# Retention and a bilinear FFN on one core: the first q load issued as two transfers of three and five heads

## The chip, the cores and the metric

The kernel runs on one core of a Trainium2 chip. The metric is device time in microseconds, the median of several executions. Beside it there is one profiled execution, whose span runs from its first to its last instruction.

## What is computed

Two stages follow each other. The first is a retention layer: for each of 8 batches and 8 heads, scores of q against k, multiplied by a causal decay, times v. The second takes the result as tokens of 512 features and runs a bilinear feed-forward network (FFN) over them.

```python
scores = scale * np.matmul(q, k.transpose(0, 1, 3, 2))    # q, k, v: (8, 8, 576, 64) float32
gamma = 1.0 - 2.0 ** (-5.0 - np.arange(H))
Dmat = np.where(rel >= 0, gamma[:, None, None] ** rel, 0.0)
attn = np.matmul(scores * Dmat, v)
x = attn.transpose(0, 2, 1, 3).reshape(B * S, H * D)      # (4608, 512)
out = ((x @ w_a) * (x @ w_b)) @ w_out                     # w_a, w_b: (512, 1536), w_out: (1536, 512)
```

Inputs and output are float32 in device memory; the products run in bfloat16, and the loads convert q, k and the weights on the way.

## The kernel before

The 4,608 tokens are worked off in blocks of 512. For each block the FFN makes, by 12 slices F of the hidden features, two products `pa` and `pb` (`ffn_ab`, L416 to L446: four products each per slice, over the four chunks of 128 input features), ACT copies `pa` to `ha`, DVE multiplies it with `pb` into `hT`, and `ffn_out` (L476) or, for block 0, `ffn_out_parts` (L458) multiplies `hT` with `wo_sb` and stores the rows. The retention of later tokens is laid between the FFN's products by a list of due times (L774 to L806), so that TensorE (PE) always has something to do.

The first 512 tokens can't be hidden in that way: there is no FFN work before them. They are handled in two units u = 0 and 1 of 256 tokens each, by functions whose names begin with `fresh_`. One load brings 256 tokens of q or k for all 8 heads: partition p gets tokens 2p and 2p+1, and for each head these two rows are one piece of 128 numbers, so one load has 128 x 8 pieces. PE then transposes by pairs of heads (`fresh_transposed`, L533), sixteen 64-wide transposes for all of q, which go through the heads in order; DVE scales the transposed q by the decay `qs0` (L669), ACT and DVE copy the transposed k (L673, L674), and PE makes scores, masks being applied by DVE, then the state and the second stage (`fresh_stage2`, L622), whose result is copied into `xT` (L646, L647) for the FFN.

All engines run their own instructions in program order. The order on GpSimd, which issues nearly all loads, is written out by hand at L161 to L171:

```python
    load_fresh_v(0, 0, 4, nc.sync)        # issued by SyncE
    load_fresh_qk(0)                      # q, then k, of tokens 0 to 255
    ramp(idx[:, 0:512], ...); ramp(posf[:, 0:4], ...); ramp(posf[:, 4:4 + MID + 1], ...)
    load_fresh_v(0, 4, 8, nc.gpsimd)
    ramp(posf[:, 4 + MID + 1:NPOS], ...)
    load_fresh_qk(1)                      # q, then k, of tokens 256 to 511
    load_fresh_v(1, 0, 8, nc.gpsimd)
    load_w(0, 128)                        # two wa and two wb loads
    load_w(128, 384)
```

The `ramp` calls make index tables on GpSimd. DVE waits for them: from `posf` and `idx` come the decay of v (`make_vs`, L195), the identity that the transposes multiply with (L211), and the masks `keep2` (`make_keep2`, L214, called at L668). ACT makes `qs0` (L206) and part of `qs` (`make_qs`, L232) from them.

PE's own order at the start is: twelve products on zeros (`idle_products`, L662), which keep it busy while the first data is on the way; the transposes of q of unit 0; two more such products; the transposes of k of unit 0; scores, state and sums of unit 0 with more such products between; the transposes of q of unit 1, one product on zeros, the transposes of k of unit 1 (L688); the second stage of unit 0; and then the FFN's first slice on tokens 0 to 255 (L698), interleaved with unit 1.

A load by GpSimd reports on one of eight semaphores in turn. From the ninth on, GpSimd waits before issuing a load until the load eight places before it has landed. In the instruction order of before this concerns the weight loads from the second `load_w` half on: the first `wb_sb` load waits for q of unit 0, the next one for k of unit 0, and the two `wb_sb` loads of `load_w(128, 384)` for k and v of unit 1.

Of the kernel before, what the change touches and what calls it, by code (L numbers as in the profile page):

```python
# [18 lines left out]
def kernel(  # L19
# [23 lines left out]
    nc = tc.nc  # L43

    B, H, S, D = q.shape
# [91 lines left out]
    def load_fresh_qk(u):  # L137
        t = [nat.tile([128, 2, DM], BF16, tag="qk", name="fqk")
             for _ in (0, 1)]
        for w, src in ((0, q), (1, k)):  # L140
            nc.gpsimd.dma_start(  # L141
                t[w].rearrange("p a b -> p (a b)").rearrange(
                    "p (h x) -> p h x", h=H),
                src[0, :, 256 * u:256 * u + 256, :].rearrange(
                    "h (p e) d -> p h (e d)", e=2))
        fresh[u] = [x.rearrange("p a b -> p (a b)").rearrange(
            "p (h e d) -> p h e d", h=H, e=2) for x in t]

# [11 lines left out]

    load_fresh_v(0, 0, 4, nc.sync)  # L161
    load_fresh_qk(0)
    ramp(idx[:, 0:512], [[1, 512]], 0, 0)
    ramp(posf[:, 0:4], [[1, 2], [256, 2]], 0, 2)
    ramp(posf[:, 4:4 + MID + 1], [[128, MID + 1]], 0, 1)
    load_fresh_v(0, 4, 8, nc.gpsimd)
    ramp(posf[:, 4 + MID + 1:NPOS], [[128, PER - MID - 1]], 64, 1)
    load_fresh_qk(1)
    load_fresh_v(1, 0, 8, nc.gpsimd)
    load_w(0, 128)  # L170
# [685 lines left out]
```

## Time and profile before

| | us |
|---|---|
| median of 5 runs | 327.53 (326.73 to 328.17) |
| the profiled execution, in all | 327.53 |
| its span | 325.7 |
| granted TensorE clock, mean | 1.000 |

The shares of busy time of the five engines, PE ahead of all, are shown with the prediction. A page of the profile gives busy time by engine, the span in 40 slices, the DMA queues, the chain of work that ended last, and the costliest groups of instructions. The timeline lists instructions by start and length; in brackets stands how long the engine was idle before and what ended that idleness. For a load that GpSimd issues, the length is that of the issue, and the landing of its data comes later.

What the early part looks like, as the timeline has it: PE's products on zeros run from 1.19 to 6.08 us, the transposes of q of unit 0 from 6.01, those of k of unit 0 from 7.70, scores from 8.80, transposes of q of unit 1 from 10.65, of k of unit 1 from 12.85, the second stage of unit 0 from 13.41, and the FFN's first product from 14.97. On the whole 23.34 MB move through GpSimd's queue and 16.95 MB through SyncE's.

### The profile page before, as it was taken

The numbers are of one execution on the slowest core, as the hardware profiler recorded it, in microseconds if no ns is written. First come the engines' busy times: TensorE is split into PE (matmuls) and PEld (weight loads), VectorE is DVE, ScalarE is ACT, GpSimd is POOL, SyncE is SP. The second block draws the span as 40 slices with busy tenths as digits, with TensorE's granted clock in tenths as the row PEclk, the third lists the DMA queues.
The fourth block names the chain that finished last, engine by engine and source line by source line (L and its number), as shares of the span: only waits on it lengthen the run. The fifth ranks groups of instructions, "written<-read, shape, count | busy, mean of one in ns | idle before, by whom it ended". The sixth has DMA issues, their size and how long they took to land.

```text
span 325.7 us, 8850 instructions
## 1 busy us (share of the span) xinstructions
PE 319.4 (98%) x3745; PEld 170.9 (52%) x3745; DVE 165.8 (51%) x329; ACT 119.3 (37%) x256; POOL 145.7 (45%) x181
## 2 busy tenths in 40 slices
PE   7899999999999999999999999999999999999996
PEld 3577757886444554455445544545444544544443
DVE  6774445856445744473636364446445634534321
ACT  5737624545034432342334143414332333313321
POOL 8696889592770565056702680098008200000000
PEclk9999999999999999999999999999999999999999
DMA  9999999999999099919991999289937850011002
GB/s 141 199 166 180 180 228 272 174 152 118 200 190 146 13 185 188 137 31 154 170 141 30 150 179 140 53 131 157 164 67 96 145 89 0 32 69 32 2 32 97
DMA packets 117383, 40.94 MB, mean 126 GB/s; under 512 B 104224, under 2 KB 110624, under 8 KB 117344
## 3 DMA queue, kind: packets, MB, share of 16 engines
q0 software_dynamic: 81824, 23.34, 69.0%
q1 hardware_dynamic: 35376, 16.95, 26.6%
q8 instruction: 29, 0.48, 0.6%
q10 hardware_dynamic: 144, 0.10, 0.1%
q14 instruction: 10, 0.08, 0.1%
HBM read 37.75 MB, written 9.44 MB: 145 GB/s over the span
## 4 chain that ended last, share of the span: by engine, by line
PE 94%; POOL 2%; DMA 2%; issue 0%; ACT 0%; POOLq 0%; ACTq 0%
PE pa L433 29%; PE pb L433 29%; PE po L497 25%; PE po L466 3%; DMA wa_sb<-in_moe_w_a_dram 2%; PE o L333 2%; PE o L386 2%; PE sc L361 2%; PE kv L294 1%; POOL fqk L141 1%; PE po L486 1%; PE tp L275 1%; POOL vf L131 0%; PE fo L628 0%; POOL idx L151 0%
## 5 line engine op out<-in xcount | busy, mean ns | idle before, releaser
L443 DVE TENSOR_TENSOR hT<-ha,pb 128x512 bf16<-128x512 bf16 (+1 forms) x123 | 76.4, 622 | 95.7 <-PE pb L433 88.8
L433 PE MATMUL pa<-xT,wa_sb 128*128 128x512 bf16 (+1 forms) x516 | 113.8, 345 | 0.3 <-DMA wa_sb<-in_moe_w_a_dram 0.2
L433 PE MATMUL pb<-xT,wb_sb 128*128 128x512 bf16 (+1 forms) x516 | 113.7, 344 | 0.0
L442 ACT CAST ha<-pa 128x512 bf16<-128x512 f32 (+1 forms) x123 | 65.5, 533 | 115.3 <-PE pa L433 114.7
L497 PE MATMUL po<-wo_sb,hT 128*128 128x512 bf16 x372 | 83.3, 379 | 0.0
L256 POOL TENSOR_TENSOR vb<-vf,vs_all 128x512 bf16<-128x512 f32 x30 | 30.8, 1042 | 101.8 <-PE o L333 94.9
L433 PEld LDWEIGHTS <-wb_sb 128*128 128x128 bf16 x516 | 50.4, 98 | 43.1
L433 PEld LDWEIGHTS <-wa_sb 128*128 128x128 bf16 x516 | 49.4, 98 | 42.3 <-DMA wa_sb<-in_moe_w_a_dram 0.5
L497 PEld LDWEIGHTS <-hT 128*128 128x128 bf16 x372 | 35.5, 98 | 41.8
L110 POOL DMA_DIRECT2D vf<-in_v_dram x36 | 31.6, 881 | 0.1
L102 POOL DMA_DIRECT2D qk<-in_q_dram x36 | 30.9, 866 | 1.2 <-DMA wo_sb<-in_moe_w_out_dram 1.1
L102 POOL DMA_DIRECT2D qk<-in_k_dram x36 | 30.9, 863 | 0.9 <-DMA wo_sb<-in_moe_w_out_dram 0.6
L316 ACT CAST sbf<-s 128x256 bf16<-128x256 f32 x56 | 22.6, 405 | 13.3 <-DVE s L307 5.4
L307 DVE TENSOR_TENSOR s<-kv,s 128x256 f32<-128x256 f32 x49 | 20.7, 423 | 11.7 <-PE kv L294 9.5
L453 DVE COPY osb<-po 128x512 f32<-128x512 f32 x17 | 11.7, 690 | 28.0 <-PE po L497 28.0
L406 DVE TENSOR_TENSOR xT<-o,qs 128x512 bf16<-128x512 f32 x32 | 20.5, 682 | 6.5 <-PE o L333 6.3
L451 ACT COPY osb<-po 128x512 f32<-128x512 f32 x18 | 10.5, 583 | 33.6 <-PE po L497 31.1
L370 DVE TENSOR_TENSOR sT<-sc,keep 128x512 bf16<-128x512 f32 x32 | 20.7, 682 | 0.0
L350 ACT CAST seen<-o 128x64 bf16<-128x64 f32 x16 | 3.4, 212 | 27.8 <-PE o L333 27.8
L333 PE MATMUL o<-qkT,sbf 64*64 64x64 bf16 x456 | 12.2, 196 | 0.0
L333 PEld LDWEIGHTS <-sbf 64*64 64x64 bf16 x456 | 8.4, 106 | 6.6 <-issue 5.9
L466 PE MATMUL po<-wo_sb,hT 128*128 128x512 bf16 x48 | 11.4, 380 | 0.0
(81 smaller groups left out, 150.7 us busy)
## 6 DMA issues: line engine op xcount, KB each, us to landing
vf<-in_v_dram POOLq DMA_DIRECT2D x29, 256.0 KB, 4.7
out_dram<-osb SPq DMA_DIRECT2D x29, 256.0 KB, 4.1
qk<-in_k_dram POOLq DMA_DIRECT2D x28, 128.0 KB, 5.7
qk<-in_q_dram POOLq DMA_DIRECT2D x28, 128.0 KB, 6.3
out_dram<-osb SPq DMA_DIRECT2D x12, 128.0 KB, 4.6
vf<-in_v_dram POOLq DMA_DIRECT2D x8, 128.0 KB, 5.5
wa_sb<-in_moe_w_a_dram POOLq DMA_DIRECT2D x4, 192.0 KB, 6.6
wb_sb<-in_moe_w_b_dram POOLq DMA_DIRECT2D x4, 192.0 KB, 7.2
```

Source lines behind the costliest of these rows:

```text
L102: nc.gpsimd.dma_start(t[r0:r0 + n, w, :].rearrange("p (h d) -> p h d", h=H), src[b, :, s0:s0 + n, :].rearrange("h s d -> s h d"))
L110: nc.gpsimd.dma_start(t[r0:r0 + n, :].rearrange("p (h d) -> p h d", h=H), v[b, :, s0:s0 + n, :].rearrange("h s d -> s h d"))
L256: eng.tensor_tensor(vb.rearrange("p (h d) -> p h d", h=H), vf.rearrange("p (h d) -> p h d", h=H), vs[:, i % PER, :].unsqueeze(2).to_broadc ...
L307: nc.vector.tensor_tensor(new, ps[s][:, ci], last_sum[0], op=ALU.add)
L316: nc.scalar.copy(sb, new)
L333: nc.tensor.matmul(o[s][half(c), ci, j, :], state_of.get(2 * i + s, zero_state)[half(r), p, :], qkt_of[i][half(r), 0, p, half(s)], start=s ...
L370: nc.vector.tensor_tensor(sT[:, r].rearrange("p n c t -> p (n c) t"), sc[r].rearrange("p n c t -> p (n c) t"), keep.unsqueeze(1).to_broadc ...
L433: nc.tensor.matmul((pa, pb)[w][:, t:t + step], (wa_sb, wb_sb)[w][:, c, fs], xT[:, c, tok0 + t:tok0 + t + step], start=(c == 0 and t == 0), ...
L442: nc.scalar.copy(ha[:, 0:n], pa[:, 0:n])
L443: nc.vector.tensor_tensor(hT[:, F, off:off + n], ha[:, 0:n], pb[:, 0:n], op=ALU.mult)
L466: nc.tensor.matmul(po[u], hT[:, F, u * 128:(u + 1) * 128], wo_sb[:, F, :], start=(F == 0), stop=(F == NF - 1))
L497: nc.tensor.matmul(po, hT[:, F, u * 128:(u + 1) * 128], wo_sb[:, F, :], start=(F == 0), stop=(F == NF - 1))
```

## The change

`load_fresh_qk(u)` issued one load of q and one of k, each for all 8 heads. Now the load of q for unit 0 is made of two, for heads 0 to 2 and for heads 3 to 7, issued one after the other from GpSimd into the two parts of the same tile. The load of k for unit 0 and both loads of unit 1 stay whole.

```diff
         for w, src in ((0, q), (1, k)):
-            nc.gpsimd.dma_start(
-                t[w].rearrange("p a b -> p (a b)").rearrange(
-                    "p (h x) -> p h x", h=H),
-                src[0, :, 256 * u:256 * u + 256, :].rearrange(
-                    "h (p e) d -> p h (e d)", e=2))
+            cuts = (0, 3, H) if (u, w) == (0, 0) else (0, H)
+            for h0, h1 in zip(cuts, cuts[1:]):
+                nc.gpsimd.dma_start(
+                    t[w].rearrange("p a b -> p (a b)")[
+                        :, 128 * h0:128 * h1].rearrange(
+                            "p (h x) -> p h x", h=h1 - h0),
+                    src[0, h0:h1, 256 * u:256 * u + 256, :].rearrange(
+                        "h (p e) d -> p h (e d)", e=2))
```

In the instruction orders of the two kernels this is one more load on GpSimd, as its second, ahead of k. PE's first transpose of q waits for the first of the two loads and its sixth for the second. The semaphores of all later loads of GpSimd move on by one place, and each load still waits for the one eight places before it. The orders on PE, DVE, ACT and SyncE are otherwise the same.

## The prediction

> **What bounds the kernel now.** I read the page's first part, then the chain of waits in order of time, then GpSimd's timeline, PE's waits, and last the stretches with DMA share and rate. PE is busy 98% of the span, and in the chain nothing but PE stands between 15 us and the end. So only the start can move the time: when PE gets its first FFN product.
>
> ```profile
> PE 319.4 (98%) x3745; PEld 170.9 (52%) x3745; DVE 165.8 (51%) x329; ACT 119.3 (37%) x256; POOL 145.7 (45%) x181
> ```
>
> The chain of waits (start, length, what) at the start:
>
> ```profile
> 1.26 1.95 POOL fqk L141 x2
> ...
> 4.98 1.71 POOL fqk L141 x2
> 6.70 0.89 POOL vf L131
> 7.58 0.57 POOL wa_sb L118
> 8.15 6.73 DMA wa_sb<-in_moe_w_a_dram
> 14.88 0.09 issue
> 14.97 0.60 PE pa L433 x4
> ```
>
> GpSimd issues one load behind another until 8.15, then the transfers take until 14.88. From 14.97 on PE hardly pauses. PE's waits in the first 40 us (total, times, longest) name the same transfers:
>
> ```profile
> PE ftp L539 <- DMA fqk<-in_k_dram: 1.7, 2, 1.2
> PE warm L655 <- DVE idle L174: 1.2, 1, 1.2
> PE pa L433 <- DMA wa_sb<-in_moe_w_a_dram: 0.2, 1, 0.2
> ```
>
> No wait for q is in that list. GpSimd's timeline shows what the added issue would push (start, length, line, target):
>
> ```profile
> 1.26 1.06 POOL L141 DMA_DIRECT2D fqk<-in_q_dram  x1 [0.81 <-POOLq L840]
> 2.31 0.90 POOL L141 DMA_DIRECT2D fqk<-in_k_dram  x1
> 3.27 0.60 POOL L151 IOTA idx<- 128x512 f32 x1
> 3.79 0.30 POOL L151 IOTA posf<- 128x4 f32 x2
> 4.00 0.81 POOL L131 DMA_DIRECT2D vf<-in_v_dram  x1
> 4.80 0.18 POOL L151 IOTA posf<- 128x4 f32 x1
> 4.88 0.93 POOL L141 DMA_DIRECT2D fqk<-in_q_dram  x1
> 5.79 0.91 POOL L141 DMA_DIRECT2D fqk<-in_k_dram  x1
> 6.66 0.93 POOL L131 DMA_DIRECT2D vf<-in_v_dram  x1
> 7.53 1.30 POOL L118 DMA_DIRECT2D wa_sb<-in_moe_w_a_dram  x2
> ```
>
> Below, q0 and k0 are the loads of the first 256 tokens, q1 and k1 those of the second, v0 the second half of v there, v1 the v of the second 256. By stretches (the last two numbers are the DMA share, which counts overlapping packets and so passes 1, and GB/s):
>
> ```profile
> 3.40:4.20 0.80, 0.80 (x4) 0.25 (x3) 0.18 (x2) 0.00 (x0) 0.80 (x4) 1.00 0.54 52
> 4.20:6.60 2.40, 2.40 (x23) 1.06 (x22) 2.16 (x10) 2.36 (x6) 2.40 (x4) 1.00 1.78 176
> ...
> 7.40:8.00 0.60, 0.30 (x10) 0.30 (x12) 0.58 (x1) 0.02 (x1) 0.60 (x2) 1.00 1.43 168
> 8.00:10.20 2.20, 2.20 (x64) 1.28 (x60) 1.82 (x5) 1.44 (x4) 2.20 (x5) 1.00 1.77 175
> ```
>
> The reader is to see a slow start to 4.2, saturation at 1.78 while q0 and k0 move, a small dip at 7.4 to 8.0 where q1 begins, and saturation again. From issue to landing the trace gives 4.7 us for q0, 5.3 for k0, 5.0 for q1, 7.0 for k1, 7.0 and 6.7 for the two parts of wa.
>
> **What the Trainium skill says.** "Perfetto Trace Analysis", section "DMA Instruction — SWDGE (GPSIMD)": the profiled length of such an issue is the generation of its descriptors, not the movement. The trace agrees: 1.06 us of issue for q0, landing 4.7 us after its start. "DMA: Bandwidth & Descriptors", section "Why a DMA increments its semaphore by 16 and not by 1": a transfer counts as landed when the last of 16 engines has reported. That fits k1: at 10.5 to 11.5 the bytes of v1 already move, yet k1 lands only at 12.8. "Perfetto Trace Analysis", section "DMA Optimizations": splitting may let work start sooner where the DMA engines are idle. The trace shows such idleness only before 4.2 us. "TensorE: Matmul & The Clock Gate", section "Part 1: The HAM clock gate", has the clock halve after an idle window of about 3.4 us; the longest wait here is 1.24 us and the granted clock is 1.00 throughout.
>
> **The change, part by part.** (1) The first issue shrinks and one is added. Three heads are 384 row pieces (128 partitions by 3), five are 640. Rows nearby: 256 pieces took 0.61 to 0.68 (wa), 384 pieces 0.78 and 640 pieces 0.89 (wo, L124), 512 pieces 0.81 (v0), 1,024 pieces 0.90 to 0.93. Bounds: 0.62 + 0.80 and 0.80 + 0.90, against 0.93 for one q issue that isn't the first: +0.49 to +0.77. I take +0.65. The wait counts of the weight loads on GpSimd move by one place: each still waits for the load eight before it, so the two wb loads that waited for k1 and v1 (1.80 and 0.88 us) still do.
>
> (2) What the early part brings. The first issue is over some 0.25 us sooner (1.06 less about 0.8), so the engines may start as much sooner. PE can't use q itself: its twelve warm-up products run from 1.19 to 6.08 and the q transposes start at 6.01, just as q0 lands at 1.26 + 4.7 = 5.95. The five heads that come second are generated by about 2.95; q0's remaining data has the engines busy beyond that. Gain in PE for q: nothing. If both parts are later than 6.08, the cover is gone and PE would pause by the difference; q0's last part can slip 0.1 us before that.
>
> (3) What slides on GpSimd by 0.65: k0's issue, three ramps, v0, q1, k1, v1, the first weight loads. The ramps feed DVE's scales (start 4.01) and through them identity and the two keep tables, then the product at L669 (start 6.76, length 1.22, end 7.98). DVE is full from 4.01 to 6.75, so L669 goes to 7.4 and ends near 8.6. The copy behind it (L674) started at 8.38, so DVE hands over the k tile some 0.25 us later. That reaches PE's scores, but PE then stands still from 11.6 to 12.85 for k1, which swallows it. ACT waited 0.73 us before L673 and so covers its 0.65. Cost on the path: nothing while k1 stays that late; 0.25 to 0.35 if k1 were on time.
>
> (4) k0: it landed 5.3 us after issue, 0.6 later than the 4.7 of the unhindered q0, because it stood behind q0 in the engines. That cover takes up the 0.65. It lands within 0.1 us of 7.65.
>
> (5) q1, the crux. It landed 5.0 us after issue; with an otherwise empty queue the same size took 4.7, of which 1.06 was the issue and not 0.93. So q1 had 0.34 us of cover counted from the start of the issue and 0.47 from its end; I take 0.40. Slide 0.65 less 0.40 = +0.25 us. Bounds: -0.25 (the engines stay fed, and the earlier start of point 2 comes through) and +0.65 (no cover at all).
>
> (6) k1, v1, wa stand in the engines behind q1, at a share of 1.77. They were issued 7.0, 7.6 and 7.0 us ahead of landing, so their own slide is covered and they inherit q1's: +0.25.
>
> (7) PE: k1's landing sets the transposes at 12.85, these set the first stage 2 at 13.41 and the copies into xT (end 14.80); wa lands at 14.88. Both arms move by +0.25, and the first product from 14.97 to 15.22. The later weight parts are needed with a margin (those issued at 17.7 to 21.5 are used from 22.96 on), so nothing is added behind that, and nothing won back, since PE has no pauses left.
>
> Sum: 0 (q) + 0 (k0) + 0.25 = +0.25, about 0.3 with the few PE gaps between 15 and 19 us. On the profiled execution 325.7 becomes 326.0. That execution took 327.53 in all, 1.8 outside its span, and is equal to the median; so 327.8.
>
> **The rivals.** The queue runs dry (slower). If q1's descriptors come after v0's bytes are through, near 7.6 us, the engines must start up anew. The start of q0 shows the price: 52 GB/s for 0.8 us in place of 176, a loss of 0.8 x (1 - 52/176) = 0.56 us. With the whole slide of 0.65 that is +1.2: 328.7. It decides from a slide of about 0.6 us upward. For it: the dip to 1.43 at 7.4 to 8.0 shows that the margin at q1 is small already. Against it: v0's own slide keeps the engines fed a little longer.
>
> The late engine catches up (faster). k1 should take about 1.5 us after q1's landing at 9.9, as q0 to k0 did (1.7), so 11.4 to 11.6; it came at 12.8, some 1.3 us behind, held by a part of the engines, while the wb loads on GpSimd waited for it. If another timing of descriptors and transfers spares it this, PE goes on from its end of the warm product, 11.6, plus the 0.3 of point 3: the first product comes near 14.0, and the wb loads unblock sooner. That gives -0.9 to -1.3, say 326.3. For it: nothing in the program makes k1 slower than q1, so the delay looks like a matter of coincidence. Against it: nothing in the change touches it either.
>
> That the change doesn't do what it says can be set aside: the instruction orders show two issues, and PE's transposes wait for the second part from the sixth on, and for nothing else new.
>
> **How the numbers follow.** Cover at q1, as worked out: 0.38, its own range 327.2 to 328.3. Dry queue: 0.35, 328.3 to 329.4. Late engine gone: 0.27, 325.9 to 326.8. The range 326.2 to 329.0 leaves out the ends of both rivals. About 0.3%, 1.0 us, is what a measurement of this kernel can tell from no change. Faster by more: 0.23 of the late engine's 0.27 and 0.02 of the first = 0.25. Slower by more: 0.31 of the dry queue's and 0.05 of the first = 0.36. Within: the rest, 0.39.
>
> **What would show it.** GpSimd's two q issues at 0.7 to 0.9 us each and every later issue until 8 us shifted by 0.5 to 0.77; q1's landing at 10.1 to 10.2; the wait of PE for k1 as long as before; the first product on wa at 15.2. A first product above 15.8, with a DMA share well under 1.4 near 7.5 to 8.3, is the dry queue; one below 14.3, with k1 landing before 12, the late engine. I am wrong altogether if the time changes while the first product stays at 14.9 to 15.3, for instance by a pause of PE behind 20 us or a granted clock under 1.

## The result and the profile after

| | before | after |
|---|---|---|
| median, us | 327.62 (326.47 to 330.31, 80 runs) | 328.58 (327.63 to 332.62, 43 runs) |
| ratio | 1 | 1.0039, interval 1.0027 to 1.0051 |
| the profiled execution, in all / its span | 327.53 / 325.7 | 329.92 / 328.1 |
| FFN's first product starts | 14.97 | 16.19 |

The medians differ by 0.96 us, or 0.29%; the ratio of the runs puts the cost at 0.39%, with an interval of 0.27 to 0.51%, some 0.9 to 1.7 us. It is small, but the interval leaves no change out. PE is still the engine that is busy nearly always:

```profile
PE 320.0 (98%) x3745; PEld 171.1 (52%) x3745; DVE 165.5 (50%) x329; ACT 119.4 (36%) x256; POOL 146.5 (45%) x182
```

PE's waits of the kernel after in the first 100 us (total, times, longest):

```profile
PE pa L436 <- DMA wa_sb<-in_moe_w_a_dram: 1.6, 1, 1.6
PE warm L658 <- DVE idle L177: 1.2, 1, 1.2
PE sc L364 <- DMA qkT<-qk: 1.2, 1, 1.2
PE ftp L542 <- DMA fqk<-in_k_dram: 1.1, 2, 0.7
```

There is still no wait for q. The wait for the weights grew from 0.2 to 1.6, and the wait for k shrank from 1.7 to 1.1. The third line lies near 71 us. It isn't part of the 0.96 us: this execution took 1.3 us more than the median of its kernel, and the experiments below whose medians are as high as this kernel's don't have it in their profiles. So of the 2.4 us by which the spans differ, 1.2 is the start, and that is the part to explain; the 1.2 of the third line isn't explained here.

The chain that ended last in the kernel after, where it leads to the first product (start, length, what):

```profile
1.26 2.74 POOL fqk L143 x3
...
5.76 1.72 POOL fqk L143 x2
7.48 0.89 POOL vf L131
8.37 0.58 POOL wa_sb L118
8.95 7.20 DMA wa_sb<-in_moe_w_a_dram
16.15 0.05 issue
16.19 0.61 PE pa L436 x4
```

It is the chain of before, with everything on GpSimd 0.8 us later (the step into the transfer at 8.95 where it was at 8.15) and the transfer itself 0.5 longer (7.20 where it was 6.73). GpSimd's timeline after:

```profile
1.26 1.83 POOL L143 DMA_DIRECT2D fqk<-in_q_dram  x2 [0.81 <-POOLq L843]
3.08 0.91 POOL L143 DMA_DIRECT2D fqk<-in_k_dram  x1
4.07 0.58 POOL L154 IOTA idx<- 128x512 f32 x1
...
5.69 0.92 POOL L143 DMA_DIRECT2D fqk<-in_q_dram  x1
6.58 0.90 POOL L143 DMA_DIRECT2D fqk<-in_k_dram  x1
7.45 0.92 POOL L131 DMA_DIRECT2D vf<-in_v_dram  x1
8.33 1.29 POOL L118 DMA_DIRECT2D wa_sb<-in_moe_w_a_dram  x2
```

The two parts of q0 take 1.83 us together, 0.92 each with a small overlap, where one issue had taken 1.06. An issue of three heads is as long as one of eight (q1, 0.92). So the slide is 0.77 at k0, 0.81 at q1 and 0.80 at the weights.

What the DMA engines did with it, by stretches (the last two numbers are the DMA share and GB/s; before had 1.48 over the first stretch, and 0.59 over the second):

```profile
2.80:10.20 7.40, 6.99 (x94) 3.27 (x93) 5.08 (x17) 4.26 (x9) 7.32 (x14) 1.00 1.31 157
3.00:4.20 1.20, 1.20 (x5) 0.37 (x4) 0.00 (x0) 0.00 (x0) 1.12 (x3) 1.00 1.02 108
4.20:6.60 2.40, 2.40 (x10) 0.74 (x10) 1.63 (x8) 1.57 (x4) 2.39 (x7) 1.00 1.41 132
7.40:8.00 0.60, 0.26 (x2) 0.00 (x0) 0.60 (x2) 0.60 (x2) 0.60 (x2) 1.00 0.87 265
8.00:8.60 0.60, 0.53 (x16) 0.48 (x16) 0.48 (x1) 0.28 (x2) 0.60 (x2) 1.00 1.16 132
8.00:10.20 2.20, 2.13 (x67) 1.56 (x68) 1.93 (x5) 1.29 (x3) 2.20 (x5) 1.00 1.41 142
```

Over 3.0 to 4.2 the share is 1.02 in place of 0.59. That doesn't show that the split starts the engines sooner: GpSimd's first packet moves at 3.06 in both kernels, and the three kernels with ramps below, which leave q0 whole, have shares of 0.49, 0.78 and 0.90 there. From 4.2 on the engines are less full than before: 1.41 where it was 1.78, and 1.41 again, from 8.0 on, where it was 1.77.

Neither the share nor GB/s can be compared alone where loads of v move among those of q and k. Two stretches of before show it, the first with q1 and k1 on the way, the second with v1:

```profile
8.40:9.20 0.80, 0.80 (x29) 0.40 (x31) 0.80 (x3) 0.80 (x2) 0.80 (x2) 1.00 1.82 180
10.80:11.40 0.60, 0.60 (x17) 0.42 (x13) 0.60 (x2) 0.41 (x3) 0.48 (x1) 1.00 1.12 391
```

Loads of v reach 391 GB/s at a share of 1.12. So the 0.87 at 265 GB/s between 7.4 and 8.0, where v0 moves, isn't as empty as it looks beside the 1.43 of before; the stretch behind it, 1.16 at 132 GB/s, is short of work (before had 1.75 and 175 from 8.0 to 8.6). Over the whole of 2.80 to 10.20 the share compares, among the kernels that differ by the slide alone: each of them moves the 64 packets of v0 there, 4 KB each, and none of v1. The share lost is (1.48 - 1.31) x 7.4 = 1.26, which at the full 1.78 is an estimated 0.7 us of transfer time. The same figure is formed for such experiments below.

### The profile page after: what moved, and what is told of

The parts are those of the page before. It is cut to its first block, busy times and chain, and to the rows that moved or that the text cites. A ratio compares the mean times of both kernels' runs of the same rounds, so it can differ in the third digit from the quotient of the medians.

```text
span 328.1 us, 8851 instructions
## 1 busy us (share of the span) xinstructions
PE 320.0 (98%) x3745; PEld 171.1 (52%) x3745; DVE 165.5 (50%) x329; ACT 119.4 (36%) x256; POOL 146.5 (45%) x182
## 4 chain that ended last, share of the span: by engine, by line
PE 91%; DMA 5%; POOL 2%; issue 0%; ACT 0%; POOLq 0%; ACTq 0%
PE pa L436 28%; PE pb L436 27%; PE po L500 25%; PE po L469 3%; DMA qkT<-qk 3%; DMA wa_sb<-in_moe_w_a_dram 2%; PE o L336 2%; PE sc L364 2%; PE o L389 1%; POOL fqk L143 1%; PE kv L297 1%; PE po L489 1%; PE tp L278 1%; POOL vf L131 0%; PE fo L631 0%
```

## The experiments

Names as in the prediction; "the slide" is the delay of GpSimd's later issues. The medians of the kernel before, in the three groups of experiments, were 327.55, 327.55 and 327.49.

**The slide without the split.** Two ramps into a spare tile, as long as one issue, stand where the added issue stood, between q0 and k0; q0 stays whole.

```diff
+            if (u, w) == (0, 0):
+                ramp(spare[:, 0:512], [[1, 512]], 0, 0)
+                ramp(spare[:, 512:768], [[1, 256]], 0, 0)
```

> The kernel before with two ramps of GpSimd (512 and 256 columns, into a table nobody reads) between the issue of q and that of k for the first 256 tokens: the same place and about the same length (0.8 to 0.9 us) as the added issue of the change, but no split. Theory A (the change costs what it pushes back on GpSimd): 0.8 to 1.2 us slower than before, like the change; k's issue near 3.2, all later issues up to 8 us pushed by 0.8 to 0.9, first FFN product on wa near 16. Theory B (two small transfers in place of one are what costs, in the DMA engines): no difference to before, within 0.3 us, first product near 15.

Measured: 328.68, ratio 1.0039 (1.0019 to 1.0058), the cost of the change. The weights' issue came at 8.37, and the share over 2.80 to 10.20 is 1.27. In the profile, whose execution was 0.85 us faster than the median, the first product started at 15.45 and not near 16. So what costs is that GpSimd is later; two transfers in place of one aren't needed for it.

**The slide further down.** The same two ramps stand ahead of q1's issue, or between q1 and k1.

```diff
+    ramp(spare[:, 0:512], [[1, 512]], 0, 0)
+    ramp(spare[:, 512:768], [[1, 256]], 0, 0)
     load_fresh_qk(1)
```

> The kernel before with the same two idle ramps on GpSimd (about 0.9 us), now ahead of q of the second 256 tokens: k, the ramps in use and v of the first 256 tokens keep their times; q and k of the second 256, v and the weights are pushed. Theory A1 (the loads of the second 256 tokens have too little cover): slower like the change, 0.8 to 1.2 us, with the DMA share of 8.0 to 10.2 us at 1.3 to 1.4 in place of 1.77. Theory A2 (what hurts is that k, the tables or v of the first 256 tokens come later): no difference, within 0.3 us.

> The same two idle ramps between q and k of the second 256 tokens. Theory A1 with the crux at q: the loads behind q stand in a full queue and have cover, so 0 to 0.4 us slower. If k has no cover either: 0.8 us and more. Theory A2: no difference.

Measured: ahead of q1 328.70, ratio 1.0039 (1.0022 to 1.0055); between q1 and k1 328.05, ratio 1.0009 (0.9992 to 1.0025). With the ramps ahead of q1, k0, the tables and v0 are issued as before, and the cost is whole; with the ramps one issue later most of it is gone by the ratio (0.3 us left, and none at all lies in the interval), though by the medians 0.50 of some 1.1 us is left. The stretches of the kernel with the ramps ahead of q1:

```profile
2.80:10.20 7.40, 6.55 (x95) 3.12 (x93) 5.77 (x18) 4.63 (x11) 7.34 (x15) 1.00 1.34 163
...
4.20:6.60 2.40, 1.88 (x22) 0.88 (x20) 2.26 (x10) 2.36 (x6) 2.40 (x5) 1.00 1.75 173
7.40:8.00 0.60, 0.31 (x12) 0.31 (x14) 0.60 (x1) 0.02 (x1) 0.60 (x2) 1.00 0.55 112
8.00:10.20 2.20, 2.20 (x64) 1.27 (x58) 1.98 (x6) 1.45 (x4) 2.20 (x5) 1.00 1.55 150
```

and with the ramps between q1 and k1:

```profile
2.80:10.20 7.40, 7.19 (x95) 3.23 (x93) 5.74 (x18) 4.51 (x10) 7.34 (x15) 1.00 1.49 178
...
8.00:10.20 2.20, 2.20 (x68) 1.39 (x63) 2.11 (x6) 1.33 (x3) 2.20 (x5) 1.00 1.72 170
```

Until 6.6 us the first of them fills the engines as before did (1.75); then, q1 being issued at 5.70, they run down to 0.55 at 112 GB/s. The expectation had looked for the gap later, as 1.3 to 1.4 from 8.0 to 10.2 (1.55). In the second, q1 is issued at 4.87 as in before, only k1, v1 and the weights are 0.8 us late, and nothing is missing: 1.49 over the whole, and the FFN's first product starts at 14.68. The weights, issued 0.8 us later, landed no later here (last part 14.59 in place of 14.88): the engines had something to do until then.

One line needs care. In the kernels with the slide alone, PE's list puts the wait ahead of the first product down to ACT's `fvb`. That product doesn't need `fvb` (in before it started at 14.97, and the first piece of `fvb` only at 15.19). PE's weight load in front of it names the real cause; for the kernel with the ramps ahead of q1, the tile `wa_sb` has these rows of what engines sat idle for, and of who waited:

```profile
  DMA wa_sb<-in_moe_w_a_dram: 2.4, 1
  ACT fvb L523: 2.1, 1
...
  PEld L436: 2.4, 1
```

The weight load waited 2.4 us for the transfer, and the product behind it started when the weights were there.

**A split where the backlog is.** v1's load, which stands behind q1 and k1, is issued in two parts of three and five heads; q0 stays whole. The same one issue more, ahead of the weights.

```diff
-    load_fresh_v(1, 0, 8, nc.gpsimd)
+    load_fresh_v(1, 0, 3, nc.gpsimd)
+    load_fresh_v(1, 3, 8, nc.gpsimd)
```

> The kernel before with another load split by three and five heads: v of the second 256 tokens, two issues behind the last load of k and ahead of wa. The added issue is as long, but only the weight loads and nothing of q and k is pushed. Theory A in its strict form (every issue ahead of wa counts in full): wa's first parts land 0.8 us later, 0.5 to 1.0 us slower. Theory A with cover as in the prediction (wa was issued 7 us ahead of landing and stands in the engines' queue): no difference, within 0.3 us. Theory B: as slow as the change, since it also has one transfer more.

Measured: 327.59, ratio 1.0008 (0.9992 to 1.0024). The chain of this kernel:

```profile
6.69 1.65 POOL vf L131 x2
8.34 0.58 POOL wa_sb L118
8.92 5.92 DMA wa_sb<-in_moe_w_a_dram
14.85 0.04 issue
14.89 0.61 PE pa L434 x4
```

The transfer starts at 8.92, as late as in the change, and takes 5.92 us in place of 7.20: the product is where it was before. Its share over 2.80 to 10.20 is 1.48, as in before. This experiment and the one before it say together: the added issue isn't dear by itself; its place ahead of q1 makes it so.

**Twice the slide.** q0 in three parts.

```diff
-            cuts = (0, 3, H) if (u, w) == (0, 0) else (0, H)
+            cuts = (0, 2, 5, H) if (u, w) == (0, 0) else (0, H)
```

> The changed kernel with q of the first 256 tokens in three parts (2, 3 and 3 heads): one more issue of about 0.9 us on GpSimd ahead of everything else. Theory A (the slide of q of the second 256 tokens on GpSimd is paid in full): about twice the loss, 1.8 to 2.4 us above before, first FFN product near 17. Rival (the loss comes from a chance late engine or one wait that was hit, and doesn't grow with the slide): as the changed kernel, about 1 us above before.

Measured: 329.61, ratio 1.0065 (1.0047 to 1.0083). GpSimd's timeline of this kernel:

```profile
1.26 2.41 POOL L143 DMA_DIRECT2D fqk<-in_q_dram  x3 [0.81 <-POOLq L843]
...
6.29 0.91 POOL L143 DMA_DIRECT2D fqk<-in_q_dram  x1
```

The slide at q1 is 6.29 less 4.88 = 1.41, and the loss 329.61 less 327.49 = 2.12 us, 1.5 per us of slide. In the change it is 0.96 on 0.81, or 1.2, and with the ramps alone 1.13 and 1.15 on 0.84 and 0.82, or 1.35 and 1.4. By the ratios it is 1.5 to 1.6 in all four. The intervals are some 0.8 us wide and more, and the lower ends for the change and for three parts are at 1.1, so a loss of exactly the slide isn't far off; what is above it stays open. The share over 2.80 to 10.20 falls to 1.16: 0.32 x 7.4 / 1.78 = 1.3 us of transfer time missing. The first product starts at 16.86; the transposes of k1, for which PE waits 1.3 us until 14.35, are late here as well as the weights.

**One figure across these kernels.** Each of the 16 DMA engines reports the end of its share of a load. The last of them scatters; the middle one (the median of the 16 records) for the second part of the first slice's `wa` (half of the partitions, so every product needs it) orders these kernels much as their times do:

| kernel | q1 issued | middle engine, second wa part | later than before | loss by medians |
|---|---|---|---|---|
| before | 4.88 | 13.07 | | |
| v1 in two parts | 4.88 | 13.10 | 0.03 | 0.04 |
| ramps between q1 and k1 | 4.87 | 13.30 | 0.23 | 0.50 |
| ramps ahead of q1 | 5.70 | 13.89 | 0.82 | 1.15 |
| the change | 5.69 | 14.08 | 1.01 | 0.96 |
| ramps ahead of k0 | 5.72 | 14.23 | 1.16 | 1.13 |
| q0 in three parts | 6.29 | 14.87 | 1.80 | 2.12 |

Each row rests on a single profile. When q1 is issued on time the weights are late by little, although their own issue is 0.8 us later; when q1 is late, they are late by about as much as the time is longer.

**Taking work off GpSimd.** If GpSimd's time is what counts, v0's issue can go to SyncE, in the kernel before and in the one after.

```diff
-    load_fresh_v(0, 4, 8, nc.gpsimd)
+    load_fresh_v(0, 4, 8, nc.sync)
```

> The kernel before, unsplit, with the second half of v of the first 256 tokens issued by SyncE. Theory A: GpSimd is 0.8 us earlier from q of the second 256 tokens on, so 0.3 to 1.0 us faster than before (less than the whole 0.8 if the DMA engines, full from 4.2 to 10 us before, then bound). Theory B says nothing of GpSimd's row: no difference.

> The changed kernel with the second half of v of the first 256 tokens issued by SyncE in place of GpSimd, which takes 0.8 us of issue out of GpSimd's row behind the split. Theory A: from q of the second 256 tokens on GpSimd is back where it was before the change (that issue at 4.9), so the time is that of before or up to 0.5 us less, since q's first part also comes earlier. Theory B: the split still costs its 1 us, so about 328.5.

Measured: 328.31, ratio 1.0015 (1.0000 to 1.0030), on the kernel before, and 328.35, ratio 1.0021 (1.0006 to 1.0037), on the one after. Both times the forecast of theory A, as fast as before or faster, failed. The relief on GpSimd comes with a new wait, here in the kernel after with v0 on SyncE:

```profile
PE ftp L542 <- DMA fqk<-in_q_dram: 1.2, 1, 1.2
```

SyncE is free at the start, so v0 goes out at once and shares the engines with q0. In the kernel before with this edit, q0 lands 6.2 us after its issue and no longer 4.7, and PE waits 1.0 us for it. Its first FFN product still starts at 14.97, as in before, so this wait doesn't explain its loss, which stays open. The pair says something else: q1 is issued at 4.08 in the unsplit and at 4.88 in the split kernel, the same slide as in the change, and the times differ by 0.04 us. The share from 8.0 to 10.2 is 1.76 and 1.78: there the engines stayed full, and the slide cost nothing that can be seen.

So next v0 was held back on SyncE, by a write of DVE to its tile, until DVE reached the masks.

```diff
-    load_fresh_v(0, 4, 8, nc.gpsimd)
...
+    nc.vector.memset(vf2[:, 0, 512:513], 0.0)
+    load_fresh_v(0, 4, 8, nc.sync)
```

> The kernel before, unsplit, with the same gated load by SyncE; q of the second 256 tokens goes out at 4.1 in place of 4.9. Theory A with the DMA engines full as the next bound (share 1.78 and 1.77 in the profile before, a dip only at 7.4 to 8.0): 0 to 0.4 us below before. If GpSimd's row alone bound: 0.8 us below.

> The changed kernel with the second half of v of the first 256 tokens issued by SyncE, held back by a one-column write of DVE ahead of the keep tables, so that it starts near 6 us, not at 1 us. GpSimd's q of the second 256 tokens goes back to 4.9 as in the kernel before, without early traffic beside q and k. Theory A: the loss is gone, 0 to 0.5 us below before. Rival (two transfers for q are what costs): still 0.8 to 1.2 us above before.

Measured: 329.93, ratio 1.0058 (1.0036 to 1.0080), on the kernel before; 331.56, ratio 1.0111 (1.0074 to 1.0149), on the one after. In the first v0 is issued at 5.30, into engines that are full (1.79 from 4.2 to 6.6), and takes 4.9 us to land; in the second it is issued at 6.1 and takes 5.2. None of the forecasts came true. PE's wait and the stretches in the first of the two (the third number from the end is the granted clock):

```profile
PE kv_sum L560 <- DVE fvb L525: 1.3, 1, 1.3
```

```profile
10.00:12.00 2.00, 0.98 (x23) 0.56 (x25) 1.73 (x4) 0.60 (x2) 0.59 (x2) 1.00 1.36 309
12.00:14.00 2.00, 2.00 (x47) 1.35 (x41) 1.16 (x3) 1.59 (x4) 0.68 (x2) 0.62 1.62 183
14.00:16.00 2.00, 2.00 (x64) 1.80 (x60) 0.79 (x2) 0.85 (x3) 2.00 (x4) 0.53 1.38 176
```

A wait of 1.3 us is followed by some 3.4 us at half the clock ((1 - 0.62) x 2 / 0.5 + (1 - 0.53) x 2 / 0.5), in which PE is full and slow. The clock isn't the whole loss: in 9 of the 15 runs of this kernel the mean granted clock was 0.993 to 0.995 and the time 329.5 to 330.4, and in five with 1.000 the time was still 328.1 to 328.8. These two kernels say nothing on what a shorter GpSimd list would bring if v0 came in time.

**Another order of the loads.** The first `wa` and `wb` loads ahead of v1, in both kernels.

```diff
-    load_fresh_v(1, 0, 8, nc.gpsimd)
     load_w(0, 128)
+    load_fresh_v(1, 0, 8, nc.gpsimd)
```

> The kernel before, unsplit, with the same exchange (weights of the first slice ahead of v of the second 256 tokens). In the profile before, xT was ready at 14.8 and wa at 14.9, so at most 0.3 us faster by wa alone; v then comes some 0.8 us later and may hold up the scaling of v (from 15.2 us): no difference to 0.5 us slower.

> The changed kernel with the four weight loads of the first FFN slice issued ahead of v of the second 256 tokens. If the late landing of wa is what the change costs (PE waited 1.6 us for it in the changed kernel, with its input xT ready at 14.6): first product at 14.6 to 15.0, time 0.8 to 1.2 us below the changed kernel, about equal to before. If the loss lies in k and the steps behind it instead: first product still near 16, no gain.

Measured: 328.79, ratio 1.0044 (1.0026 to 1.0062), and 329.61, ratio 1.0064 (1.0043 to 1.0085). On the kernel before, the FFN's first product now starts at 13.94, 1.0 us earlier, but then PE waits for v1, at 16.76:

```profile
PE kv_sum L561 <- DVE fvb L526: 1.1, 1, 1.1
```

On the kernel after, the first product came at 15.70 and not by 15.0, and the time is 1.0 us above that of the change, not below it. The weights were there (14.43), but PE had waited for k0 and k1 (2.4 us in all, the transposes of k1 at 13.61), and `xT` came late. So the weights aren't the only thing on which the start can hang behind the split.

**q1 early, the split kept.** q1's issue moves to directly behind k0, ahead of the ramps and v0, in the kernel after.

```diff
     load_fresh_qk(0)
+    load_fresh_qk(1, (0,))
...
-    load_fresh_qk(1)
+    load_fresh_qk(1, (1,))
```

> The changed kernel with q of the second 256 tokens issued right behind k of the first, ahead of the ramps and of v; its issue moves from 5.7 to 4.0, ramps and v come 0.9 us later still. Theory A with the crux at q of the second 256: the loss of the change is gone, within 0.4 us of before or below. If the total of GpSimd's issues ahead of k and v of the second 256 is what counts, and not q's place: as the changed kernel, about 1 us above before, or more as DVE's tables come 1.7 us later than before.

Measured: 328.56, ratio 1.0031 (1.0015 to 1.0048), no relief. q1 is issued at 3.99, yet the tables and v0 come later by one issue, and PE waits 0.9 us for v0's product. The time is the one forecast for the case that the total of the issues counts and not q1's place. But the moved load put a new wait into the place of the old, so this doesn't test the place of q1 alone. In the profiled execution the clock halves as above (0.72 from 12 to 14, 0.50 from 14 to 16); in the other 21 runs the mean granted clock was 0.999 or 1.000, so the median doesn't come from that.

No version was quicker than the kernel before; the split behind q1 is level with it.

## Why the prediction was right and wrong

The time lies within the range, but the likeliest case isn't the one that came. The sum for that case, 327.8, was too low by 0.8 us, and the range holds because it was drawn across most of a rival's. What came is that rival, "the queue runs dry": forecast 328.7, its marks a first product above 15.8 (it is 16.19) and a share well under 1.4 near 7.5 to 8.3 (0.87, though v0's packets lower it; 1.16 right behind). Its point of decision, a slide of about 0.6 us, was passed.

- Step (1), the added issue: mis-sized. It took +0.65 from rows by number of pieces, with an upper bound of +0.77; measured +0.77 at k0 and +0.81 at q1. The assumption that failed is that an issue with fewer pieces is shorter: 0.92 for three heads, 0.92 for eight. Only that the first issue shrinks was right (1.06 falls to 0.92), so the added issue costs 0.92 less 0.14.
- Step (2), no gain and no wait for q: right, though the engines didn't start sooner as it allowed for (first packet at 3.06 before and after). The parts of q0 landed at 1.26 + 3.3 = 4.6 and 2.17 + 4.2 = 6.4 us. The second is some 0.4 later than the 5.95 of before, more than the 0.1 allowed, and the transposes of q started at 6.42 in place of 6.01. Yet PE's list shows no wait for q: in this execution the products on zeros last until then (the first twelve took 5.30 us in place of 4.89). With the ramps in place of the split they start at 6.42 too, so this isn't the split's doing, and what follows waits for k0 anyway.
- Steps (3) and (4), tables, DVE and k0 at nothing: right in effect. Ramps ahead of k0 and ramps ahead of q1 cost the same (1.13 and 1.15 us), so k0, tables and v0 being late adds nothing to the loss that these intervals show. PE's scores started at 9.18 in place of 8.80, and the wait for k1 took that up, as foreseen. DVE wasn't quite full before (2.16 of the 2.40 us from 4.2). That k0 lands within 0.1 of 7.65 wasn't met (8.03).
- Step (5), the crux, is the step at which the likeliest case failed: mis-sized. It deducted a cover of 0.40 at q1, from 5.0 us of landing less the 4.7 of a load into an otherwise empty queue. q1 took 5.0 from issue to landing again, so it landed at 10.7 in place of 9.9, the whole slide of 0.8 late. The cover was nil in this profile, although in before the engines stood at a share of 1.43 when q1 began. With the ramps q1 took 4.7 (ahead of q1) and 5.4 (ahead of k0), and 5.4 with three parts, so one profile fixes the cover to no better than about 0.4. q0's own 4.7 contain its slow start, so they are no measure of a load without delay.
- Step (6), k1, v1 and the weights covered and all later by q1's +0.25: half right. That a slide behind q1 is covered, in the main, two experiments bear out (share 1.49 and 1.48, ratios 1.0009 and 1.0008). But what they inherit from q1 isn't 0.25: by the middle engine the weights' second part arrived at 14.08 in place of 13.07, 1.0 later.
- Step (7), both arms move: wrong for k1. k1's transposes started at 12.66 where they had started at 12.85. The middle engine was done with k1 at 11.83 in place of 10.85, but the last at 12.62 in place of 12.80: the lag of the last engine, on which the faster rival rested, was smaller at k1, without gain, because one was late at the weights instead (last engine 16.15, the one ahead of it 14.87, middle 14.08). The last engine scatters from profile to profile (first products at 15.45 and 15.87 in the two kernels with the ramps that have the same median). By the middle engine about 1.0 of the 1.2 us in the profile is the change; that the rest is chance isn't shown. Nor is it known what holds the last engine up.

The dry queue's own sum, 0.65 of slide and 0.56 for a new start of the engines, came near the total by other terms, which is luck. The slide alone is 0.8. A new start at 52 GB/s wasn't seen in the change (132 from 8.0 to 8.6); the engines ran at part load for 2.2 us from 8.0, at a share of 1.41, with k1 issued since 6.58. Why they weren't full then isn't settled by these runs.

The Trainium skill, "Perfetto Trace Analysis", section "DMA Optimizations", says that splitting may let some transfers start sooner. The trace agrees for the first part, which landed at 4.6 us in place of 5.95 for the whole; the second came at 6.4, PE's transposes began no sooner, and every load behind was issued 0.8 us later.

## What to carry to other kernels

Cutting a load that GpSimd issues costs the queue behind it nearly a full issue: here 0.8 us, for parts of three and five heads. Put such an issue only where the DMA engines have a backlog: look at the DMA share of the stretches in which the loads behind it begin to move, and don't count on cover where it dips (1.43 at q1 here, and no cover was left). Compare the share over the whole start between two kernels; among the kernels that differ by the slide alone it told 0 from 0.6 to 0.9 and 1.3 us of lost transfer time. It doesn't rank kernels whose loads are issued otherwise: with v0 on SyncE it was 1.58, above the 1.48 of before, and the kernel was no faster. Where the last landing of a single profile scatters by half a microsecond and more, take the middle engine's.

## What the hardware showed beyond this

- The length of an issue was 0.92, 0.92 and 0.92 us for three, five and eight heads of q; three issues of two, three and three heads took 2.41, or 0.80 each.
- The granted clock fell to a half for some 3.4 us after waits of 0.9 to 1.5 us, in the profiles of three kernels, while waits of 1.24 us in before and about 2.1 us with the ramps ahead of q1 left it at 1.00. The Trainium skill, "TensorE: Matmul & The Clock Gate", section "Part 1: The HAM clock gate", speaks of an idle window of about 3.4 us that doesn't start with the kernel. Here far less idleness was enough, in an interval in which PE was half busy (0.98 of the 2 us from 10 to 12, as far as its records go); the phase of such a window may decide it, which no run tested.
- One such fall takes about 0.005 off the mean granted clock of a run (0.5 x 3.4 / 328, an estimate). A mean of 0.995 or less stands in 6 of the 43 runs of the change, in 9 of 15 with v0 held back on SyncE in the kernel before, and in 7 of 186 of the kernel before itself. In the change these are runs of 330.2 us and more.
